# One of the four later modulation rows: its products on ScalarE, its sum by accumulating DMAs

## The chip, the cores and the metric

The kernel runs on one core of a Trainium2 chip. A core has a matrix engine (TensorE, PE in the profile), a vector engine (VectorE, DVE), an engine for pointwise functions (ScalarE, ACT), a programmable engine (GpSimd, POOL) and a sequencer that only issues transfers (SyncE, SP). Each takes its instructions strictly in order. Data lies in HBM, in the on-chip memory SBUF (128 partitions) and in PSUM, where TensorE writes its sums. DMA engines move data between HBM and SBUF, or from one place in SBUF to another; here SyncE and GpSimd issue all of them, and a transfer issued by GpSimd may also add what it brings to what already lies at its destination.

The metric is the time of one execution on the device in microseconds (us), lower being better. The profiler counts a span, from the first to the last instruction.

## The reference

```python
mod = (silu(c) @ w_mod).reshape(c.shape[0], 6, 1, -1)    # c: (1, 1024), w_mod: (1024, 6*1024)
sa, ca, ga, sb, cb, gb = (mod[:, i] for i in range(6))
h = layernorm(x) * (1 + ca) + sa                          # x: (1, 2048, 1024)
a = einsum("bsd,ed->bse", h, dft_hid_re)
b = einsum("bsd,ed->bse", h, dft_hid_im)
y = einsum("ts,bse->bte", dft_seq_re, a) - einsum("ts,bse->bte", dft_seq_im, b)
x = x + ga * y
h = layernorm(x) * (1 + cb) + sb
x = x + gb * (gelu(layernorm(h) @ w1 + b1) @ w2 + b2)     # w1: (1024, 3584), w2: (3584, 1024)
```

Six rows of 1024 numbers come from the vector c. The first two (sa, ca) are needed before the Fourier mixing, and the other four (ga, sb, cb, gb, numbered j = 2 to 5) only behind it. This case is about the row ga, j = 2.

## The kernel before

Every large product is made in 16-bit floats: each operand is split into a high half (ScalarE rounds it) and a low half (VectorE subtracts the rounded value), and three products of halves are summed. Where it can, the kernel forms seven products of sums of blocks in place of eight plain block products (Strassen's and Winograd's scheme); VectorE makes those sums.

The work follows in stages. First the rows sa and ca and the first normalization. Then the Fourier mixing along the sequence: `plain1` handles the first of four blocks of 512 outputs with 16 operands of plain products (L1123), `winograd1` the other three (tb = 1, 2, 3; L1173) with seven products of four operands each, 28 operands to a block and 84 in all, 24 matmuls to an operand. Then mixing along the hidden dimension (L1405), and the two products of the gated network (L1600, L1709).

In the second stage several streams of small tasks run beside TensorE:

- `craw` and `op`: SyncE loads pieces of the sequence matrices (L716). `split_c` turns each into an operand: the high half on ScalarE (L692), the low half on VectorE (L695). A ring of six places holds finished operands, and a place is free again when TensorE is through with its operand. Four of the seven products need sums of raw pieces first (`comb`, L727).
- `s` and `sr`: sums of the normalized input, split (L669, L672), stored in HBM by GpSimd (L676) and reloaded by SyncE (L754) into a ring of four; a reload waits until TensorE has used the place.
- `u`: the results, evicted from PSUM by ScalarE (L1192) or VectorE (L1197), combined and split (L799, L784, L787) in a staging ring of three, and stored by GpSimd (L789).
- `row`: the four later modulation rows, one after the other (`row_tasks`), and behind them, in the same stream, eight units `d_tasks` that load a part of the hidden-dimension matrices (`dre`, `dim`; L821), split it (L832 on ScalarE, L835 on VectorE) and store it (L839).

A row is made like this. Eight pieces of 128 rows of `w_mod` (128 x 1024 floats, 512 KB) are loaded by SyncE into a ring of three buffers (L547). Each is multiplied by its column of silu(c) (`scol`), one factor for each partition, and summed into `mrow` by VectorE: the first by L553, the other seven by L555. GpSimd then adds up the 128 partitions (`partition_all_reduce`, L563), VectorE scales or shifts the row (`keep`: L567 for ga, L569 for cb; `keep_b2`, L574, for the product of gb with b2), and GpSimd stores it in HBM (`put`, L577). There is one `mrow`, so the next row's first product waits until the store has read it. The first `dre` load lies over the same space and waits for the last store, that of `gbb`.

The order of all this is written down when the program is built. A small planner keeps a clock for each engine. `Task` has an engine, an estimated cost and the tasks it depends on; `push` puts tasks in a stream with a time at which they fall due; `pick` takes the task that is due first among those that could start at once on their engine, and otherwise the one that could start earliest. The operands fall due 15 us ahead of their use, the rows at fixed times 30 us apart, the units of `d_tasks` 24 us apart. `LANDS` says how long a transfer is taken to need, 2 us for a load. The planner's estimates set only the order on each engine; the waits on the chip are those of the data.

Of the kernel before, what the change touches and what calls it, by code (L numbers as in the profile page):

```python
# [12 lines left out]
AF = mybir.ActivationFunctionType  # L13
ALU = mybir.AluOpType
# [21 lines left out]
def kernel(ctx, tc, x, cre, cim, dre, dim, w1, b1, w2, b2, c, wm, out):  # L36
# [13 lines left out]
    pe, act, dve, gp, sp = nc.tensor, nc.scalar, nc.vector, nc.gpsimd, nc.sync  # L50

    pool = ctx.enter_context(tc.tile_pool(name="main", bufs=1))
# [6 lines left out]
    def mk(shape, dt, tag, bufs=1):  # L59
        cnt[0] += 1  # L60
        return pool.tile(shape, dt, tag=tag, name=f"{tag}_{cnt[0]}", bufs=bufs)
# [3 lines left out]
    def at(kb, n, dt=F32):  # L65

        w = n if dt == F32 else n // 2
        v = arena[:, int(kb * 256) : int(kb * 256) + w]
        return v if dt == F32 else v.bitcast(dt)
# [92 lines left out]
    acc = at(O_ACC, 8192).rearrange("p (b j r e) -> p b j r e", b=2, j=2, r=2)  # L162
# [54 lines left out]
    LANDS = {"dma": 2.0, "st": 4.0, ("st", "d"): 7.0, ("st", "u"): 5.0, ("st", "s"): 4.0, ("st", "z"): 4.0}  # L217
# [142 lines left out]
    def level():  # L360
        t = max(clk.values())
        for k in clk:
            clk[k] = t
        return t
# [100 lines left out]
    scol, cc = mk([P, ND], F32, "scol"), mk([P, ND], F32, "cc")  # L465
    m1 = mk([P, 6], F32, "m1")
    srep = at(216, 1024).rearrange("p (k m) -> p k m", k=ND)
    mrow, ones = at(O_AUX, 1024), at(O_SO[0], 512)
# [25 lines left out]
    def mod_rows(k, c_lo, x1):  # L494
# [43 lines left out]
        lo(1)  # L538
        dve.tensor_scalar(iu, pm, 2.0**5 / SD, None, op0=ALU.mult)

    def row_tasks(j, name):

        r = []
        for k in range(ND):
            b = at(O_AUX + 4 + 4 * (k % 3), 1024)
            l = Task(
                "dma", 1.5, lambda k=k, b=b: sp.dma_start(b, wm[:, k, j * D : (j + 1) * D]),  # L547
                [("row", j, k - 3) if k > 2 else ("row", j - 1, ND) if j > 2 else ("op", 15)], ("wm", j, k),
            )

            def mul(k=k, b=b):
                if k == 0:
                    dve.tensor_scalar(mrow, b, scol[:, 0:1], None, op0=ALU.mult)  # L553
                else:
                    dve.scalar_tensor_tensor(mrow, b, scol[:, k : k + 1], mrow, op0=ALU.mult, op1=ALU.add)  # L555

            r.append((l, Task("dve", 1.3, mul, [l.key], ("row", j, k))))
        t = [l for l, _ in r[:3]]
        for k in range(ND):
            t.append(r[k][1])  # L560
            if k + 3 < ND:
                t.append(r[k + 3][0])
        s = Task("pool", 7.0, lambda: gp.partition_all_reduce(mrow, mrow, P, RED.add), [("row", j, ND - 1)])  # L563

        def keep():
            if name == "ga":
                dve.tensor_scalar(mrow, mrow, m1[:, 3:4], None, op0=ALU.mult)  # L567
            elif name == "cb":
                dve.tensor_scalar(mrow, mrow, 1.0, None, op0=ALU.add)  # L569

        b = at(O_AUX + 4, 1024)

        def keep_b2():
            dve.tensor_tensor(mrow, mrow, b, op=ALU.mult)  # L574

        def put(n, dep, key=None):
            return Task("st", 0.0, lambda: gp.dma_start(row_d[n][:, :], mrow), [dep], key)  # L577

        if name == "gb":
            l = Task("dma", 1.5, lambda: sp.dma_start(b, b2[0].partition_broadcast(P)), [s.key])  # L580
            p = put("gb", s.key)
            m = Task("dve", 1.3, keep_b2, [l.key, p.key])
            return t + [s, l, p, m, put("gbb", m.key, ("row", j, ND))]
        if name == "sb":
            return t + [s, put(name, s.key, ("row", j, ND))]
        k_ = Task("dve", 0.9, keep, [s.key])
        return t + [s, k_, put(name, k_.key, ("row", j, ND))]
# [921 lines left out]
    for n, j in enumerate((2, 3, 4, 5)):  # L1509
        push("row", "row", row_tasks(j, {2: "ga", 3: "sb", 4: "cb", 5: "gb"}[j]), t_op(16) + 20.0 + 30.0 * n)  # L1510
# [308 lines left out]
    due, t = {}, 0.0  # L1819
# [4 lines left out]
    t = level()  # L1824
# [174 lines left out]
```

## Time and profile before

| | |
|---|---|
| median of three runs | 1976.67 us (1975.83 to 1977.92) |
| profiled execution | 1976.73 us |
| its span | 1975.0 us |
| TensorE busy | 1954.2 us, 99% |
| VectorE busy | 1422.2 us, 72% |
| ScalarE busy | 851.7 us, 43% |
| GpSimd busy | 196.3 us, 10% |
| TensorE's granted clock | 0.997 |

In the lines of the profile, L with a number is a line of the kernel. "Busy" of TensorE counts overlapping, pipelined matmuls, so that it says little on its speed. A row of the timeline gives the start of a group of instructions in microseconds from the span's start, how long the group took, the engine, the line, the operation with its output and input, how many instructions it joins, and in brackets how long the engine had been idle before, and what ended that. `SPq`, `POOLq` and the like are the sequencers that issue transfers. A row of the view of one line gives the shortest, the median and the longest duration in nanoseconds and the first and the last start; "DMA to landing" is the time from issuing a transfer until its data lies at its destination, shortest, median and longest. Almost all data on the chip lies in one tile, `arena`; names like `in_wm_dram`, `s`, `u`, `dc` and `row_ga` are tensors in HBM.

### The profile page before, as it was taken

What the parts mean: (1) busy time and instruction counts of PE and PEld (TensorE: products, weight loads), DVE (VectorE), ACT (ScalarE), POOL (GpSimd) and SP (SyncE); (2) the same over time, 40 slices, a digit from 0 to 9 for tenths busy, and PEclk for the clock granted to TensorE, in tenths of its full rate; (3) what the DMA queues carried; (4) which work ended last, traced back from release to release, by engine and by line L of the source; (5) the groups of instructions that cost most, each with busy time, mean ns of one, the idle gap of its engine ahead of it and who ended that gap; (6) DMA issues with size and microseconds to landing.
All of it is one profiled execution on the core that took longest, in us unless ns stands there. A gap on an engine that the chain in (4) does not pass through costs nothing.

```text
span 1975.0 us, 23586 instructions
## 1 busy us (share of the span) xinstructions
PE 1954.2 (99%) x9004; PEld 889.2 (45%) x9004; DVE 1422.2 (72%) x1799; ACT 851.7 (43%) x1091; POOL 196.3 (10%) x287
## 2 busy tenths in 40 slices
PE   7999999999999999999999999999999999999999
PEld 2444444444444444444444444444444444444443
DVE  5977878797985477786689998989873453553566
ACT  3843333354542255554577566456323312312311
POOL 0012212221210012211020000000000000000000
PEclk9999999999999999999999999999999999999999
DMA  9148587598778867878954554444476432432324
GB/s 385 62 142 283 183 299 289 210 330 312 268 271 335 302 241 252 288 234 298 357 177 150 189 189 164 149 149 176 171 224 197 123 102 74 130 103 67 113 75 85
DMA packets 139362, 402.41 MB, mean 204 GB/s; under 512 B 15536, under 2 KB 15536, under 8 KB 134640
## 3 DMA queue, kind: packets, MB, share of 16 engines
q1 hardware_dynamic: 111808, 307.30, 46.1%
q0 software_dynamic: 27440, 93.60, 13.3%
q8 instruction: 70, 1.15, 0.2%
q14 instruction: 44, 0.36, 0.1%
HBM read 262.95 MB, written 137.89 MB: 203 GB/s over the span
## 4 chain that ended last, share of the span: by engine, by line
PE 92%; DVE 4%; ACT 1%; issue 1%; DMA 1%; POOL 0%; SPq 0%; DVEq 0%; ACTq 0%; POOLq 0%
PE ps L1600 24%; PE ps L1173 22%; PE ps L1709 22%; PE ps L1405 15%; PE ps L1123 8%; DVE arena L409 1%; DVE arena L1755 1%; PE ps L485 1%; PE ps L1307 1%; DVE arena L422 1%; ACT arena L397 1%; DMA arena<-in_w_dram 0%; DMA arena<-in_wm_dram 0%; DVE arena L1799 0%; PE ps L484 0%
## 5 line engine op out<-in xcount | busy, mean ns | idle before, releaser
L1709 PE MATMUL ps<-arena 128*128 128x512 f16 x2352 | 511.1, 379 | 2.9 <-DVE arena L1755 1.6
L1600 PE MATMUL ps<-arena 128*128 128x512 f16 x2352 | 510.2, 379 | 0.0
L1173 PE MATMUL ps<-arena 128*128 128x512 f16 x2016 | 435.3, 379 | 0.0
L1709 PEld LDWEIGHTS <-arena 128*128 128x128 f16 x2352 | 229.8, 98 | 281.9 <-issue 4.0
L1600 PEld LDWEIGHTS <-arena 128*128 128x128 f16 x2352 | 230.2, 98 | 276.8
L1755 DVE SCALAR_TENSOR_TENSOR arena<-ps,i4c,arena 128x1024 f32<-128x1024 f32 x179 | 229.3, 1281 | 144.6 <-PE ps L1709 142.6
L1173 PEld LDWEIGHTS <-arena 128*128 128x128 f16 x2016 | 197.3, 98 | 237.9
L1405 PE MATMUL ps<-arena 128*128 128x512 f16 x1344 | 292.2, 379 | 0.0
L397 ACT ACTIVATE arena<-arena,shc 128x512 f16<-128x512 f32 (+1 forms) x115 | 116.1, 1018 | 281.6 <-PE ps L1709 189.2
L1405 PEld LDWEIGHTS <-arena 128*128 128x128 f16 x1344 | 131.5, 98 | 155.9
L1123 PE MATMUL ps<-arena 128*128 128x512 f16 x768 | 171.4, 386 | 6.8 <-ACT arena L528 3.9
L422 DVE TENSOR_TENSOR arena<-arena 128x512 f32<-128x512 f32 (+1 forms) x228 | 170.9, 753 | 4.2
L692 ACT ACTIVATE arena<-arena 128x1024 f16<-128x1024 f32 x100 | 103.8, 1050 | 152.2 <-PE ps L1173 101.1
L409 DVE SCALAR_TENSOR_TENSOR arena<-arena,shc 128x512 f16<-128x512 f32 (+1 forms) x115 | 128.6, 1122 | 37.4 <-ACT arena L397 37.1
L695 DVE SCALAR_TENSOR_TENSOR arena<-arena 128x1024 f16<-128x1024 f32 x100 | 132.7, 1345 | 22.8 <-ACT arena L692 22.6
L1626 DVE TENSOR_TENSOR arena<-arena,ps 128x512 f32<-128x512 f32 x84 | 57.6, 685 | 109.9 <-PE ps L1600 106.2
L1619 ACT ACTIVATE arena<-arena,b1s,i1c 128x512 f32<-128x512 f32 x84 | 68.3, 813 | 137.8 <-DVE arena L1626 137.8
L1123 PEld LDWEIGHTS <-arena 128*128 128x128 f16 x768 | 76.0, 99 | 102.6 <-issue 9.7
L784 ACT ACTIVATE arena<-arena 128x1024 f16<-128x1024 f32 x56 | 57.5, 1047 | 50.9 <-DMA u<-arena 19.3
L787 DVE TENSOR_TENSOR arena<-arena 128x1024 f16<-128x1024 f32 x56 | 66.8, 1217 | 14.9 <-ACT arena L784 14.9
L397 ACT ACTIVATE arena<-arena,s1c 128x512 f16<-128x512 f32 (+1 forms) x70 | 60.7, 884 | 38.1 <-DVE arena L422 26.3
L409 DVE SCALAR_TENSOR_TENSOR arena<-arena,s1c 128x512 f16<-128x512 f32 (+1 forms) x70 | 66.4, 959 | 10.8 <-ACT arena L397 10.8
(167 smaller groups left out, 1395.1 us busy)
## 6 DMA issues: line engine op xcount, KB each, us to landing
w<-arena SPq DMA_DIRECT2D x64, 512.0 KB, 4.9
arena<-w SPq DMA_DIRECT2D x119, 256.0 KB, 2.8
u<-arena POOLq DMA_DIRECT2D x56, 512.0 KB, 5.8
arena<-u SPq DMA_DIRECT2D x112, 256.0 KB, 4.2
arena<-w SPq DMA_DIRECT2D x56, 512.0 KB, 3.6
arena<-s SPq DMA_DIRECT2D x48, 512.0 KB, 6.4
arena<-in_cre_dram SPq DMA_DIRECT2D x32, 512.0 KB, 7.4
arena<-in_cim_dram SPq DMA_DIRECT2D x32, 512.0 KB, 5.0
```

Of the source, the lines that this page charges most:

```text
L397: act.activation(o[m][0], q(j), AF.Copy, **sc)
L409: dve.scalar_tensor_tensor(o[m][1], q(j), scale, o[m][0], op0=ALU.mult, op1=ALU.subtract)
L422: dve.tensor_tensor(q(d), q(a), q(b), op=op)
L692: h = Task("act", 1.15, lambda: act.activation(o[:, :, 0], s2, AF.Copy, scale=SC), list(deps) + free)
L695: dve.scalar_tensor_tensor(o[:, :, 1], s2, SC, o[:, :, 0], op0=ALU.mult, op1=ALU.subtract)
L1123: pe.matmul(bank_of(d_), hleft(d_, s, kp, a), cop(n)[:, s, b], start=(kp == 0 and s == 0 and a == 0 and b == 0), stop=(kp == 7 and s == 1 ...
L1173: pe.matmul(bank_of(st + ch), left, cop(n)[:, s, b], start=(start and kp == 0 and s == 0 and a == 0 and b == 0), stop=(kp == 3 and s == 1 ...
L1405: pe.matmul(bank_of(bk), up(N)[:, c_, a], dp(n)[:, c_, w], start=(start and ri == 0 and c_ == 0 and i == 0), stop=(ri == 1 and c_ == 3 and ...
L1600: pe.matmul(ps.rearrange("p (k t) -> p k t", k=4), w1c[:, m, s, a, d * P : (d + 1) * P], zc(m)[:, b, :, d, :], start=(start and d == 0 and ...
L1619: act.activation(dst, src, AF.Gelu_apprx_tanh, scale=inv, bias=b1s[:, 2 * p + j : 2 * p + j + 1])
L1709: pe.matmul(t[:, j], hidc[:, c_, m, a, k * P : (k + 1) * P], w2c[:, m, c_, w], start=(start and c_ == 0 and n == 0), stop=(c_ == 1 and n = ...
L1755: lambda: dve.scalar_tensor_tensor(dst, ps[b], inv, dst, op0=ALU.mult, op1=ALU.add), kp[b],
```

## The change

For the row j = 2 alone, `scaled` takes the place of the eight VectorE instructions. ScalarE multiplies a piece by its column of silu(c): the first into `mrow`, the other seven in place in their buffers. GpSimd then issues, for each of the seven, a DMA that adds the buffer to `mrow`. Each waits for its product and for the DMA before it. A buffer is free for its next load when the DMA that reads it has landed. The planner is told 1.1 us for a product on ScalarE, 1 us for issuing an accumulating DMA and 8 us for its landing. The row's all-reduce, scaling and store, and the other three rows, are made as before.

```diff
+    def scaled(acc, b, k, name, dep):
+
+        key = lambda k: (*name, k)
+        LANDS[key(k)] = 8 if k else 0.0
+        if k == 0:
+            return [Task("act", 1.1, lambda: act.activation(acc, b, AF.Copy, scale=scol[:, k : k + 1]), [dep], key(k))]
+        p = (*name, k, "b")
+        return [
+            Task("act", 1.1, lambda: act.activation(b, b, AF.Copy, scale=scol[:, k : k + 1]), [dep], p),
+            Task("pool", 1.0, lambda: gp.dma_start(acc, b, accum_op=ALU.add), [key(k - 1), p], key(k)),
+        ]
+
     def row_tasks(j, name):
...
                 [("row", j, k - 3) if k > 2 else ("row", j - 1, ND) if j > 2 else ("op", 15)], ("wm", j, k),
             )
 
+            if j in (2,):
+                r.append((l, scaled(mrow, b, k, ("row", j), l.key)))
+                continue
+
             def mul(k=k, b=b):
...
-            r.append((l, Task("dve", 1.3, mul, [l.key], ("row", j, k))))
+            r.append((l, [Task("dve", 1.3, mul, [l.key], ("row", j, k))]))
         t = [l for l, _ in r[:3]]
         for k in range(ND):
-            t.append(r[k][1])
+            t += r[k][1]
             if k + 3 < ND:
                 t.append(r[k + 3][0])
```

Sixteen lines are added, so lines from about 560 on have numbers larger by 12, and from 565 on by 16: L695 becomes L711, L1173 becomes L1189. As built, the orders on all engines but TensorE differ from those before from about the middle of the stores of s until the last `dc` loads; TensorE's order is the same.

## The prediction

> **What bounds the kernel now.** I read the page's busy shares first, then the chain that ended last, cut to the stretch in which the change works (the queue orders of the two programs agree before about 185 us and after about 610 us, and TensorE's order is the same throughout), then VectorE's, GpSimd's and SyncE's timelines there.
>
> ```profile
> span 1975.0 us, 23586 instructions
> PE 1954.2 (99%) x9004; PEld 889.2 (45%) x9004; DVE 1422.2 (72%) x1799; ACT 851.7 (43%) x1091; POOL 196.3 (10%) x287
> 184.83 27.63 PE ps L1123 x128
> 212.46 435.12 PE ps L1173 x2016
> 647.58 12.52 PE ps L1405 x58
> ```
>
> The chain there is TensorE alone, without a gap: 2016 matmuls in 435.12 us. They use 84 operands, prepared by ScalarE (L692) and VectorE (L695), so one operand lasts 435.12 / 84 = 5.18 us, and operand j (from 0) is wanted at 212.46 + 5.18 j. Nothing that this change frees can shorten that row; it can only lengthen it, by making an operand late. So what counts is how early operands are ready now. I counted the L695 rows of the timeline to number them; three of the latest:
>
> ```profile
> 390.98 1.23 DVE L574 TENSOR_TENSOR arena<-arena 128x1024 f32<-128x1024 f32 x1 [9.37 <-issue]
> 393.26 1.22 DVE L695 SCALAR_TENSOR_TENSOR arena<-arena 128x1024 f16<-128x1024 f32 x1
> 435.40 1.22 DVE L695 SCALAR_TENSOR_TENSOR arena<-arena 128x1024 f16<-128x1024 f32 x1
> 442.42 1.22 DVE L695 SCALAR_TENSOR_TENSOR arena<-arena 128x1024 f16<-128x1024 f32 x1 [1.14 <-ACT arena L692]
> ```
>
> They are operands 36, 44 and 45, ended at 394.5, 436.6 and 443.6 and wanted at 398.9, 440.4 and 445.6: 4.4, 3.8 and 2.0 us to spare. Ahead of the first, VectorE stood 9.37 us for the last row's all-reduce; the other two lie behind pieces of the `dre` splits (L835), which follow the rows in their stream. The rows' lateness is passed on to these places.
>
> **The change, part by part.** Off VectorE go one product of L553 and seven of L555; onto ScalarE come eight activations, priced as the nearest (L692, also 1024 elements).
>
> ```profile
> L553 DVE TENSOR_SCALAR arena<-arena,scol x4: 743/746/754, 217.5 to 349.0; 128x1024 f32<-128x1024 f32 x4
> L555 DVE SCALAR_TENSOR_TENSOR arena<-arena,scol x28: 1275/1283/1285, 220.4 to 370.1; 128x1024 f32<-128x1024 f32 x28
> L692 ACT ACTIVATE arena<-arena x100: 1039/1056/1058, 28.3 to 616.5; 128x1024 f16<-128x1024 f32 x100
> ```
>
> That is 0.75 + 7 x 1.28 = 9.7 us less on VectorE and 8 x 1.06 = 8.4 us more on ScalarE, both beside a full TensorE: worth nothing by themselves. ScalarE's cover is the operand lead; were it gone, at most 8.4 us would show.
>
> The seven accumulating DMAs are issued by GpSimd, each after the one before has landed. The trace has no such DMA into SBUF; the nearest add 512 KB into HBM from the same queue:
>
> ```profile
> L1808 POOL DMA_DIRECT2D out_dram<-arena x8: 845/1066/1537, 1463.9 to 1490.5; - x8
> DMA to landing us min/median/max: 6.4/10.1/13.1
> ...
> L1783 POOL DMA_DIRECT2D out_dram<-arena x4: 1191/1198/1201, 1940.6 to 1962.8; - x4
> DMA to landing us min/median/max: 5.6/5.7/5.8
> ```
>
> 5.7 us one by one, up to 13.1 in a burst. I take 9: ours are one by one, but beside busy DMA engines. In GpSimd's order two go between the stores of s, the other five behind the last:
>
> ```profile
> 211.49 1.07 POOL L676 DMA_DIRECT2D s<-arena  x2 [0.82 <-DVE arena L672]
> 235.17 7.02 POOL L563 PARTITION_ALL_REDUCE arena<-arena  x1 [22.61 <-DVE arena L555]
> 295.10 7.28 POOL L563 PARTITION_ALL_REDUCE arena<-arena  x1
> 331.67 7.00 POOL L563 PARTITION_ALL_REDUCE arena<-arena  x1 [28.34 <-DVE arena L555]
> 379.17 8.42 POOL L563 PARTITION_ALL_REDUCE arena<-arena  x1
> ...
> 388.00 0.55 POOL L577 DMA_DIRECT2D row_gb<-arena  x1 [0.41 <-POOL arena L563]
> 392.62 0.55 POOL L577 DMA_DIRECT2D row_gbb<-arena  x1 [4.08 <-DVE arena L574]
> ```
>
> From 212.6, and some 3 us for stores pushed back, the five end at 216 + 5 x 9 = 261 and the all-reduce at 268 (now 242.2). VectorE comes to the row's scaling (L583 after) at about 266, and the next operand behind it, 16, is wanted at 295.3: no cost at 5.7 (251.5), nor at 13.1 (288.5). SyncE's queue waits too: the reloads of the ring wait for landings, with raw c loads behind that are wanted from 254 on, and the stores of u behind the chain have a ring of three. All this stays inside the lead.
>
> [...] In the trace issuing took 0.85 to 1.54 us (L1808).
>
> The cost comes later, from where the planner has put the three other rows. SyncE's order:
>
> ```profile
> 305.74 1.08 SPq L754 DMA_DIRECT2D arena<-s  x2
> 341.99 0.33 SPq L754 DMA_DIRECT2D arena<-s  x1
> ...
> 395.61 0.56 SPq L821 DMA_DIRECT2D arena<-in_dre_dram  x1
> ...
> 430.05 10.68 SPq L754 DMA_DIRECT2D arena<-s  x3
> ```
>
> Row sb's last wm load now stands behind the reload at 305.74, cb's behind the one at 341.99; these wait for TensorE. Loads of wm landed thus:
>
> ```profile
> L547 SPq DMA_DIRECT2D arena<-in_wm_dram x4: 407/423/454, 342.4 to 352.8; - x4
> DMA to landing us min/median/max: 5.1/8.8/9.9
> ...
> L547 SPq DMA_DIRECT2D arena<-in_wm_dram x4: 328/328/367, 358.0 to 366.5; - x4
> DMA to landing us min/median/max: 3.4/4.8/7.1
> ```
>
> Row sb: 306.5 + 7 (between the medians) + 1.3 = 314.8, all-reduce to 322 (now 302.4). Row cb: 342.4 + 8.8 + 1.3 = 352.5; its all-reduce now follows three stores of u, whose halves and two operands lie on VectorE in between (5 x 1.2 = 6): 359 to 366 (now 331.7 to 338.7). Then 0.7 for the scaling and nine instructions of 1.2 to gb's first product, which ends at 377 (now 349.8, below).
>
> ```profile
> 349.03 0.74 DVE L553 TENSOR_SCALAR arena<-arena,scol 128x1024 f32<-128x1024 f32 x1
> 367.48 3.92 DVE L555 SCALAR_TENSOR_TENSOR arena<-arena,scol 128x1024 f32<-128x1024 f32 x3
> ...
> 234.98 6.69 DVE L695 SCALAR_TENSOR_TENSOR arena<-arena 128x1024 f16<-128x1024 f32 x2
> ```
>
> gb now takes 349.0 to 371.4, 22.4 us. With three buffers and lighter transfers (4.8) I get 16.5: last product 393.6. Its all-reduce starts at once, to 400.7, and holds VectorE, as at 234.98: 6.69 for two instructions of 1.22, so 4.3 us. One combination and operand 36 lie there: 393.6 + 1.2 + 4.3 + 1.2 = 400.3, wanted at 398.9. **Stall 1.4 us.**
>
> Then four instructions and the b2 product to 406.3, the store of gbb (0.2 + 2.9 to land), and the first `dre` load, which waits for it:
>
> ```profile
> DMA to landing us min/median/max: 2.9/2.9/6.9
> ...
> DMA to landing us min/median/max: 5.6/7.8/9.9
> ...
> 403.47 0.68 DVE L835 SCALAR_TENSOR_TENSOR arena<-arena 128x512 f16<-128x512 f32 x1
> ...
> 418.16 1.22 DVE L695 SCALAR_TENSOR_TENSOR arena<-arena 128x1024 f16<-128x1024 f32 x1
> ```
>
> The first line is of L577, the second of L821. Load at 410 (now 395.6), landed 418; VectorE is free at 420.7 after 12 instructions. The splits up to the next operand took 403.47 to 419.4, 15.9: so 436.6 or a little more. That is operand 43, wanted at 435.2 plus the 1.4 lost: **0.5**. Operand 44 follows after four instructions and a ScalarE half, 5.9: 443.1 against 440.4 + 1.9: **0.8**. The second `dre` load stands behind the second reload of that block (430.05) and lands at 441, in time. Operand 45 takes 5.7 more, 448.8 against 445.6 + 2.7: **0.5**; operand 46 6.7 more, 455.5 against 450.7 + 3.2: **1.6**. Operand 47 is in time again. The sum is 4.8 us: 1976.73 in the profiled execution (1975.0 of span and 1.7 around it; the median of the three runs is 1976.67) becomes 1981.5.
>
> ```profile
> L835 DVE SCALAR_TENSOR_TENSOR arena<-arena x32: 678/1216/1227, 403.5 to 576.3; 128x1024 f16<-128x1024 f32 x24, 128x512 f16<-128x512 f32 x8
> ...
> 680.43 0.60 SPq L1524 DMA_DIRECT2D arena<-row_ga  x1
> ```
>
> The finished rows are read back only at 680, and the `dre` chain, which ends at 577.5 and would end some 15 to 20 us later, still frees its buffer before 600 for loads wanted from 647.58 on: no cost.
>
> **Rivals.** *Not slower (0.38).* Every stall above is a difference of two long sums. With wm landings of 4.8 in row cb too, each step is 4 us earlier, operand 36 is done at 396.3 before 398.9, and about 1 us is left: 1976.7 to 1979. For it: VectorE's own 9.7 us less. Against it: the spare time is 2 to 4 us already. It decides when gb's last product ends before 392.
> *Slow accumulation (0.10).* If a step takes over 14 us, 216 + 5 x 14 + 7 = 293 and VectorE stands at the scaling while operand 16 is wanted at 295.3; each us more costs 5. At 15.5 it is about 8 us, with later stalls 1988. Against it: 13.1 is the most seen, in a burst. [...]
> *Faster, or nothing done (0.02).* A gain needs a gap in TensorE's row, and there is none; if VectorE still ends each row by waiting, its freed time is idle time.
>
> **How the numbers follow.** Stalls of 3 to 9 us 0.50, slow accumulation 0.10, not slower 0.38, faster 0.02. The bound between slower and same is 0.2%, 4 us, about what a measurement of this kernel can tell from no change; I count 0.02 of the first case below it. So slower 0.58, same 0.40, faster 0.02. The range runs from no stall, 1976.0, to landings of 8.8 also in gb (4 us on each of two rounds, near 1985) and row ga at 13.1 (some 4 more): 1989. The likeliest case alone: 1979.7 to 1986.
>
> **What would show it.** Right: idle TensorE before L1189 (now L1173) between 395 and 460 us, ended by L711; VectorE waiting at L590 and before L711 there; an all-reduce of row gb ending near 400; accumulations 6 to 13 us apart; nothing changed after 650 but the shift. Wrong: no idle TensorE at all; gb's all-reduce before 392; or the gap near 295, behind L583.

## The result and the profile after

The changed kernel takes 1981.3 us (median of 11 runs, 1977.6 to 1984.15) against 1976.65 us (median of 11, 1974.31 to 1979.18): a ratio of 1.0023, with a 95% interval of 1.0015 to 1.0031. It is slower by 0.23%, 4.65 us; forecast were 1981.5 us and slower. The profiled execution took 1980.01 us. The first lines are from its page, the others from TensorE's timeline:

```profile
span 1978.1 us, 23589 instructions
PE 1952.5 (99%) x9004; PEld 888.4 (45%) x9004; DVE 1411.3 (71%) x1791; ACT 859.8 (43%) x1099; POOL 199.8 (10%) x294
```

```profile
212.59 233.63 PE L1189 MATMUL ps<-arena 128*128 128x512 f16 x1081
447.93 5.34 PE L1189 MATMUL ps<-arena 128*128 128x512 f16 x24 [1.71 <-DVE arena L711]
453.75 196.78 PE L1189 MATMUL ps<-arena 128*128 128x512 f16 x911 [0.48 <-DVE arena L711]
650.38 9.88 PE L1421 MATMUL ps<-arena 128*128 128x512 f16 x45
```

VectorE has 10.9 us less work and ScalarE 8 us more (9.7 and 8.4 were forecast). The row of 2016 matmuls, which had no gap before, has two, of 1.71 and 0.48 us, at operands 45 and 46, both ended by VectorE's low halves (L711). From the first matmul of L1189 to the first of L1421 it takes 650.38 - 212.59 = 437.79 us in place of 435.12: 2.67 us more. That stage length is the yardstick below. It is finer than the whole time, since the moment at which the stage begins differs between executions: 209.47 to 212.59 us over all profiles, and these two are of kernels whose orders agree up to there (e9_splits_behind below, and after).

GpSimd's timeline, the view of L550 (the accumulating DMA) and VectorE's timeline show the rows on their way:

```profile
L550 POOL DMA_DIRECT2D arena<-arena x7: 848/871/903, 186.4 to 249.5; - x7
...
DMA to landing us min/median/max: 4.5/6.8/10.1
```

```profile
260.97 6.15 POOL L579 PARTITION_ALL_REDUCE arena<-arena  x1
315.15 7.00 POOL L579 PARTITION_ALL_REDUCE arena<-arena  x1 [43.56 <-DVE arena L571]
356.48 7.28 POOL L579 PARTITION_ALL_REDUCE arena<-arena  x1
391.93 7.01 POOL L579 PARTITION_ALL_REDUCE arena<-arena  x1 [6.30 <-DVE arena L571]
```

```profile
392.88 5.55 DVE L711 SCALAR_TENSOR_TENSOR arena<-arena 128x1024 f16<-128x1024 f32 x1
...
437.69 1.22 DVE L711 SCALAR_TENSOR_TENSOR arena<-arena 128x1024 f16<-128x1024 f32 x1
442.11 0.69 DVE L851 SCALAR_TENSOR_TENSOR arena<-arena 128x512 f16<-128x512 f32 x1 [3.20 <-ACT arena L848]
...
446.66 1.22 DVE L711 SCALAR_TENSOR_TENSOR arena<-arena 128x1024 f16<-128x1024 f32 x1
...
452.48 1.23 DVE L711 SCALAR_TENSOR_TENSOR arena<-arena 128x1024 f16<-128x1024 f32 x1
```

The four all-reduces start at 261, 315, 356 and 392 us; before, it was 235, 295, 332 and 379. The gaps come from the last block above. At 438.9 VectorE is through with operand 44 (the row of 437.69). Next in its order is the first split of the second `dre` unit (L851), and it stands 3.20 us for that. The low halves of operands 45 and 46 (446.66, 452.48) stand behind it. What it waits for is ScalarE's half of that split (L848), and ScalarE stands for the unit's load itself, with the high half of operand 45 (L708) behind it. ScalarE's timeline:

```profile
441.45 1.58 ACT L848 ACTIVATE arena<-arena 128x512 f16<-128x512 f32 x2 [7.25 <-DMA arena<-in_dre_dram]
...
444.74 1.05 ACT L708 ACTIVATE arena<-arena 128x1024 f16<-128x1024 f32 x1
```

That high half is done at 445.8, when TensorE wants it (212.59 + 45 x 5.18 = 445.7); the low half at 447.9. So one late load holds both engines that make operands. SyncE's timeline, first of the kernel after, then of the one before, tells why the load was late:

```profile
425.16 5.50 SPq L770 DMA_DIRECT2D arena<-s  x2
430.76 0.55 SPq L837 DMA_DIRECT2D arena<-in_dre_dram  x1
```

```profile
414.94 1.42 SPq L821 DMA_DIRECT2D arena<-in_dre_dram  x1
```

In the order of after it stands behind two more reloads of s that wait for TensorE to free their places, and goes out at 430.76, 16 us later than before. The chain of waits has how long it took to land:

```profile
430.76 10.61 DMA arena<-in_dre_dram
```

The same load took 9.4 us in the kernel before; at that, by an estimate, it would have landed at 440.2 here, still behind 438.9. So it is mostly the late issue that counts.

### The profile page after: what moved, and what is told of

Read it like the earlier page. It is cut to its first block, busy times and chain, and to the rows that moved or that the text cites. A ratio compares the mean times of both kernels' runs of the same rounds, so it can differ in the third digit from the quotient of the medians.

```text
span 1978.1 us, 23589 instructions
## 1 busy us (share of the span) xinstructions
PE 1952.5 (99%) x9004; PEld 888.4 (45%) x9004; DVE 1411.3 (71%) x1791; ACT 859.8 (43%) x1099; POOL 199.8 (10%) x294
## 4 chain that ended last, share of the span: by engine, by line
PE 86%; DVE 8%; DMA 2%; issue 2%; ACT 1%; POOL 1%; SPq 0%; DVEq 0%; ACTq 0%; POOLq 0%
PE ps L1616 25%; PE ps L1725 23%; PE ps L1189 16%; PE ps L1421 15%; PE ps L1139 5%; DVE arena L711 1%; DMA arena<-in_wm_dram 1%; DVE arena L660 1%; DMA arena<-in_dre_dram 1%; DVE arena L661 1%; PE ps L485 1%; POOL arena L579 1%; PE ps L1323 1%; DVE arena L1771 1%; DVE arena L663 1%
## 5 line engine op out<-in xcount | busy, mean ns | idle before, releaser
L1189 PE MATMUL ps<-arena 128*128 128x512 f16 x2016 | 435.8, 379 | 2.2 <-DVE arena L711 2.2
L1189 PEld LDWEIGHTS <-arena 128*128 128x128 f16 x2016 | 197.3, 98 | 240.5 <-issue 3.0
L1421 PE MATMUL ps<-arena 128*128 128x512 f16 x1344 | 292.2, 379 | 0.0
L1421 PEld LDWEIGHTS <-arena 128*128 128x128 f16 x1344 | 131.5, 98 | 155.9
L708 ACT ACTIVATE arena<-arena 128x1024 f16<-128x1024 f32 x100 | 103.4, 1050 | 143.1 <-PE ps L1189 99.4
L711 DVE SCALAR_TENSOR_TENSOR arena<-arena 128x1024 f16<-128x1024 f32 x100 | 130.8, 1327 | 37.8 <-ACT arena L708 37.8
L803 DVE TENSOR_TENSOR arena<-arena 128x1024 f16<-128x1024 f32 x56 | 66.8, 1219 | 17.7 <-ACT arena L800 17.7
```

The costliest lines, as they stand in the source:

```text
L708: h = Task("act", 1.15, lambda: act.activation(o[:, :, 0], s2, AF.Copy, scale=SC), list(deps) + free)
L711: dve.scalar_tensor_tensor(o[:, :, 1], s2, SC, o[:, :, 0], op0=ALU.mult, op1=ALU.subtract)
L1189: pe.matmul(bank_of(st + ch), left, cop(n)[:, s, b], start=(start and kp == 0 and s == 0 and a == 0 and b == 0), stop=(kp == 3 and s == 1 ...
L1421: pe.matmul(bank_of(bk), up(N)[:, c_, a], dp(n)[:, c_, w], start=(start and ri == 0 and c_ == 0 and i == 0), stop=(ri == 1 and c_ == 3 and ...
```

## The experiments

Two things can have moved that load: the real time that the sums need, or the order that the planner wrote when it was told of 8 us for each. "Lost" in this table is the stage length less 435.12 us, from TensorE's timeline in the run's profile; the ratio is to the kernel before on the same chip.

| run | edit | lost, us | ratio (95% interval) |
|---|---|---|---|
| after | | 2.67 | 1.0023 (1.0015 to 1.0031) |
| e1_no_sum | after without the seven sums | 4.69 | 1.0026 (1.0015 to 1.0036) |
| e2_dve_same_plan | order of after, row ga on VectorE | 4.96 | 1.0025 (1.0014 to 1.0037) |
| e7_no_gb_reduce | after without gb's all-reduce | 4.75 | 1.0020 (1.0011 to 1.0028) |
| b1_gb_reduce_twice | before, gb's all-reduce twice | 4.03 | 1.0023 (1.0014 to 1.0032) |
| e5_dve_add | ScalarE's products, VectorE's sums | 5.74 | 1.0033 (1.0020 to 1.0046) |
| e6_unit1_later | after, second `dre` unit loaded later | 0.29 | 1.0041 (1.0029 to 1.0053) |
| e9_splits_behind | after, that unit's splits behind operand 46 | 0.00 | 0.9998 (0.9989 to 1.0007) |
| e3_lands2 | after, planner told 2 us a sum | 9.73 | 1.0065 (1.0052 to 1.0078) |
| e4_sum_twice | after, each sum issued twice | 21.83 | 1.0138 (1.0118 to 1.0158) |
| e10_before_plan | work of after, planned as before | 15.93 | 1.0086 (1.0072 to 1.0099) |
| b2_plan_128, b6_plan_133 | before, another figure for the planner | 0.00, 0.00 | 1.0000 (0.9991 to 1.0009), 0.9996 (0.9988 to 1.0005) |

### Is it the sums, or the order? e1_no_sum and e2_dve_same_plan

```diff
-            Task("pool", 1.0, lambda: gp.dma_start(acc, b, accum_op=ALU.add), [key(k - 1), p], key(k)),
+            Task("pool", 1.0, lambda: None, [key(k - 1), p], key(k)),
```

> The seven accumulating DMAs are left out (row ga is then only its first product, so the result is not the reference's); the order on every queue, as the planner wrote it with 8 us a landing, is that of the kernel after. Theory A (the written order costs it: the last wm loads of rows sb and cb stand on SyncE behind reloads that wait for TensorE, so gb ends late whatever row ga does): row ga is done by 240, yet sb's all-reduce still starts near 315, gb's near 390, and TensorE still idles 2 to 6 us between 395 and 460; 1979 to 1983. Rival B (the real landings of the sums hold the rows up, or their traffic slows the loads): no idle TensorE, 1976 to 1977.5.

In the second run the planner's tasks stay, and what they issue is changed:

```diff
-            return [Task("act", 1.1, lambda: act.activation(acc, b, AF.Copy, scale=scol[:, k : k + 1]), [dep], key(k))]
+            return [Task("act", 1.1, lambda: dve.tensor_scalar(acc, b, scol[:, 0:1], None, op0=ALU.mult), [dep], key(k))]
...
-            Task("act", 1.1, lambda: act.activation(b, b, AF.Copy, scale=scol[:, k : k + 1]), [dep], p),
-            Task("pool", 1.0, lambda: gp.dma_start(acc, b, accum_op=ALU.add), [key(k - 1), p], key(k)),
+            Task("act", 1.1, lambda: None, [dep], p),
+            Task("pool", 1.0, lambda: dve.scalar_tensor_tensor(acc, b, scol[:, k : k + 1], acc, op0=ALU.mult, op1=ALU.add), [key(k - 1), p], key(k)),
```

> The planner plans the kernel after, but what is issued for row ga are the eight VectorE instructions of before, at the places where ScalarE's first product and the seven sums stood. No ScalarE product, no accumulating DMA, result as the reference's. Theory A (written order): as after, 1979 to 1983, gb's all-reduce near 390. Rival B (the DMAs' landings or traffic) and rival C (ScalarE's 8 x 1.13 us push back the high halves): 1976 to 1977.5, no idle TensorE between 395 and 460.

TensorE's timeline of the first:

```profile
209.83 233.26 PE L1189 MATMUL ps<-arena 128*128 128x512 f16 x1080
444.07 0.38 PE L1189 MATMUL ps<-arena 128*128 128x512 f16 x1 [0.97 <-ACT arena L708]
446.15 203.65 PE L1189 MATMUL ps<-arena 128*128 128x512 f16 x935 [1.71 <-DVE arena L711]
649.64 50.67 PE L1421 MATMUL ps<-arena 128*128 128x512 f16 x234
```

In the second the two gaps are 1.24 and 1.71 us, at the same places. Without one accumulating DMA, and even without ScalarE's products, the loss is there, at the same operand 45 (1080 matmuls are 45 operands of 24), in both halves now: its high half (L708) comes 0.97 us late, its low half 1.71 us after that. The high half is late because ScalarE, too, stood for the load: it went out at 428.00, and ScalarE's half of its split (L848) let VectorE go on only at 440.33, after 5.50 us. So the sums' landings, their traffic and ScalarE's 8 us are not what costs; the written order is. One number of the first expectation missed: row ga's all-reduce began at 258.22, not before 240, since in GpSimd's order it stands behind stores of u, whoever made the row.

### Is it row gb's lateness? e7_no_gb_reduce, b1_gb_reduce_twice, e5_dve_add

```diff
-        s = Task("pool", 7.0, lambda: gp.partition_all_reduce(mrow, mrow, P, RED.add), [("row", j, ND - 1)])
+        s = Task("pool", 7.0, lambda: gp.partition_all_reduce(mrow, mrow, P, RED.add) if j < 5 else None, [("row", j, ND - 1)])
```

> The kernel after without the all-reduce of row gb (gb is then only a sum over the rows of one partition, so the result is not the reference's). The row is stored some 7 us earlier, VectorE isn't held, and the first dre load goes out 5 to 7 us earlier. Theory (lateness is handed from row gb to the dre units): idle TensorE under 0.5 us, 1976 to 1978. Rival (places behind row gb lose their slack by something else, ScalarE or traffic): as after, 1979 to 1982.

The theory fell here. SyncE's timeline of that run:

```profile
401.92 0.56 SPq L837 DMA_DIRECT2D arena<-in_dre_dram  x1
...
422.21 5.50 SPq L770 DMA_DIRECT2D arena<-s  x2
427.80 0.99 SPq L837 DMA_DIRECT2D arena<-in_dre_dram  x1
```

The first `dre` load goes out at 401.92 instead of 410.49, 8.6 us earlier. Of these, 3.0 us are the stage, which began at 209.63 instead of 212.59; counted from its start the first load is 5.6 us earlier, and the second not at all: 218.17 us behind the start in both, since it stands behind the reloads, and these go at TensorE's pace. VectorE stood 6.11 us for it instead of 3.20, and 4.75 us are lost. What was gained ahead was waited away at that place.

The 5.6 us need not be the all-reduce's: in e9_splits_behind, which has the all-reduce and the same order up to there, the first load is as early (192.3 us behind the stage's start, 197.9 in after). Over the profiles of after and of four runs with its order there (e1, e2, e7, e9) the first load goes out 192.3 to 197.9 us behind the start, and the second at 218.2 each time.

In the kernel before, on the other hand, where the second load goes out 16 us earlier, a late row is enough:

```diff
-        s = Task("pool", 7.0, lambda: gp.partition_all_reduce(mrow, mrow, P, RED.add), [("row", j, ND - 1)])
+        s = Task("pool", 7.0, lambda: [gp.partition_all_reduce(mrow, mrow, P, RED.add) for _ in range(1 + (j == 5))], [("row", j, ND - 1)])
```

> The kernel before, with row gb's all-reduce issued twice in a row (gb is then 128 times too large, so the result is not the reference's): row gb is 7 us later by nothing else, no ScalarE product and no accumulating DMA. Theory (a late gb row is enough, since operands 36, 44, 45 have 2 to 4.4 us to spare): VectorE held twice, operand 36 ready at 400 to 402 for 398.9, and TensorE idles 1.5 to 6 us between 398 and 460; 1978 to 1983. Rival (it needs the sums or their order): 1976 to 1977.5.

TensorE's timeline:

```profile
397.44 41.60 PE L1173 MATMUL ps<-arena 128*128 128x512 f16 x192 [0.84 <-DVE arena L695]
441.30 5.34 PE L1173 MATMUL ps<-arena 128*128 128x512 f16 x24 [2.25 <-DVE arena L695]
447.10 201.96 PE L1173 MATMUL ps<-arena 128*128 128x512 f16 x935 [0.46 <-DVE arena L695]
```

Operand 36 is the first that is late, 44 and 45 follow: the three tight places that the prediction quoted of the kernel before. So the mechanism that it described is real; it is just not the one that ended last in the order of after.

The third run keeps ScalarE's products, with no accumulating DMA and so a short row ga:

```diff
-        LANDS[key(k)] = 8 if k else 0.0
+        LANDS[key(k)] = 0.0
...
-            Task("pool", 1.0, lambda: gp.dma_start(acc, b, accum_op=ALU.add), [key(k - 1), p], key(k)),
+            Task("dve", 1.3, lambda: dve.tensor_tensor(acc, acc, b, op=ALU.add), [key(k - 1), p], key(k)),
```

> Row ga's products stay on ScalarE, but VectorE adds them (seven TENSOR_TENSOR of 1.22 us) and no accumulating DMA is issued; the planner is told so, and its order of the three other rows is again near that of before. Theory (ScalarE's 8 products of 1.13 us cost nothing; the loss needs row ga to be long): gb's all-reduce between 375 and 385, no idle TensorE over 0.5 us, 1976 to 1978. Rival C (the products on ScalarE hold up the high halves): idle TensorE between 185 and 300 behind L708, over 1979.

Wrong as well: row gb's all-reduce starts at 375.76, earlier than before (379.17), there is no late high half, and yet 5.74 us are lost. TensorE's and VectorE's timelines:

```profile
454.26 5.34 PE L1189 MATMUL ps<-arena 128*128 128x512 f16 x24 [3.32 <-DVE arena L711]
```

```profile
448.44 0.69 DVE L851 SCALAR_TENSOR_TENSOR arena<-arena 128x512 f16<-128x512 f32 x1 [4.81 <-ACT arena L848]
```

It is the third `dre` unit here, loaded at 436.14, for which VectorE stands 4.81 us with operand 46 behind it; another 1.42 us are lost at operand 38, behind the splits of the first unit. Neither a sum nor a late row is needed: a `dre` split ahead of an operand that is wanted soon, and its load behind the reloads, do it.

### The place itself: e9_splits_behind and e6_unit1_later

```diff
-        first = split((0,), slice(0, 1), [l.key]) + split((1, 5), slice(2, 4), [l.key])
+        first = split((0,), slice(0, 1), [l.key] + ([("op", 62)] if n == 1 else [])) + split((1, 5), slice(2, 4), [l.key])
```

The kernel counts the 16 operands of the first block too, so its `op` 62 is operand 46.

> The kernel after, with one dependency more in the plan: the second dre unit is loaded when it was, but its first split waits in the plan for operand 46 and so stands behind operands 45 and 46 in VectorE's order. Theory (all of the idle TensorE is VectorE waiting for that unit's load with 45 and 46 behind it, and the sums of row ga cost nothing): idle TensorE under 0.5 us between 395 and 460; the last unit ends before 605, so that the dc loads behind 650 wait for under 1 us; 1976 to 1978, not told from before. Rival (the units are as late as in the run that loaded the second one later): 2 us or more of idle TensorE behind 650 for dc, 1979 to 1984.

SyncE's, VectorE's and TensorE's timelines of it:

```profile
427.63 1.17 SPq L837 DMA_DIRECT2D arena<-in_dre_dram  x1
```

```profile
436.23 1.22 DVE L711 SCALAR_TENSOR_TENSOR arena<-arena 128x1024 f16<-128x1024 f32 x1
...
439.75 1.22 DVE L711 SCALAR_TENSOR_TENSOR arena<-arena 128x1024 f16<-128x1024 f32 x1
441.48 0.69 DVE L851 SCALAR_TENSOR_TENSOR arena<-arena 128x512 f16<-128x512 f32 x1 [0.51 <-ACT arena L848]
```

```profile
209.47 435.28 PE L1189 MATMUL ps<-arena 128*128 128x512 f16 x2016
```

The load goes out when it did in the run without gb's all-reduce (427.80), and its split starts no earlier (441.48, there 440.19). But VectorE makes operands 45 and 46 meanwhile, at 436.23 and 439.75, and ScalarE their high halves ahead of the split as well. No gap is left: 1976.38 us, ratio 0.9998. All engines' orders are those of after up to that split. With the sums, ScalarE's products and the long row ga all in place, the change costs nothing measurable. That settles the cause: the two engines waiting for that load with operands 45 and 46 behind them. How much of it is ScalarE's wait and how much VectorE's, this run can't tell, since it moves both.

Loading the unit later instead moves the lateness on:

```diff
-        l = Task("dma", 2.9, lambda: sp.dma_start(b, dri[ri][:, c_::4, :]), [("dd", n - 1)] if n else [("row", 5, ND)])
+        l = Task("dma", 2.9, lambda: sp.dma_start(b, dri[ri][:, c_::4, :]), [("dd", n - 1)] + ([("op", 62)] if n == 1 else []) if n else [("row", 5, ND)])
```

> The kernel after with one dependency more in the plan: the second dre unit is loaded only once operand 46 is ready, so that its splits stand behind operands 45 and 46 and no more ahead of them. Theory (the idle TensorE of 1.7 and 0.5 us sits at operands 45 and 46 because VectorE waits for that unit's late load in front of them): none of it left there, 1976 to 1978, if the units, then some 20 us later, still end before their buffer is wanted. Rival (VectorE lacks time there whatever stands ahead; or the loss is noise of the start): idle TensorE moves to neighbouring operands, 1979 to 1983.

TensorE's waits behind 600 us:

```profile
PE ps L1421 <- DMA arena<-dc: 5.1, 2, 3.5
```

The gaps at 45 and 46 are gone (0.29 us lost). But the units now run from 446.52 to a last load at 598.46, and TensorE waits 5.1 us for `dc` in the next stage: 1985.02 us. The prediction had put "no cost" on a `dre` chain 15 to 20 us later. With the last load at 573.28, as in the kernel after, that held; 25 us more broke it.

### What late sums would cost: e3_lands2, e4_sum_twice, e10_before_plan

```diff
-        LANDS[key(k)] = 8 if k else 0.0
+        LANDS[key(k)] = 2 if k else 0.0
```

> The kernel after with the planner told 2 us instead of 8 for the landing of a sum. The scaling of row ga (L583) then stands in VectorE's order ahead of operand 8, wanted near 254. Theory A with the measured step of 8 to 10 us a sum: the seventh sum lands at 248 to 255, the all-reduce ends at 255 to 262, VectorE stands there, TensorE idles 3 to 12 us near 254 to 270, and 1980 to 1990 with what comes later. Rival (the loss comes only from the long landing that the planner was told, and a plan with a short one is as good as before): 1976 to 1977.5, no idle TensorE near 254.

VectorE's timeline, then TensorE's:

```profile
251.58 0.75 DVE L583 TENSOR_SCALAR arena<-arena,m 128x1024 f32<-128x1024 f32 x1 [17.95 <-POOL arena L579]
```

```profile
253.52 20.66 PE L1189 MATMUL ps<-arena 128*128 128x512 f16 x95 [1.99 <-DVE arena L711]
278.30 39.23 PE L1189 MATMUL ps<-arena 128*128 128x512 f16 x168 [4.11 <-DMA arena<-s]
```

VectorE stands 17.95 us for row ga at the scaling, as the slow case of the prediction has it, and TensorE 1.99 us behind it, less than the 3 to 12 us expected. The larger gap is one that I had not listed: 4.11 us for a reload of s.

```diff
-            Task("pool", 1.0, lambda: gp.dma_start(acc, b, accum_op=ALU.add), [key(k - 1), p], key(k)),
+            Task("pool", 1.0, lambda: [gp.dma_start(acc, b, accum_op=ALU.add) for _ in range(2)], [key(k - 1), p], key(k)),
```

> Each accumulating DMA is issued twice, one after the other (the sum counts seven products twice, so the result is not the reference's); the planner's order is that of after. The five sums behind the stores of s take 85 us instead of 45: the last lands near 296, the all-reduce ends near 303, and the scaling stands ahead of operand 16, wanted at 295.5. By the prediction's third case (from 14 us a step on, each us costs 5): idle TensorE of 8 to 14 us near 295 to 310 behind L583, and rows sb, cb, gb some 30 us later with more idle behind: 1988 to 2015. Rival (sums are pipelined by the queue and a second one costs far less than the first): the scaling before 285, 1979 to 1984.

The total, 2003.1 us, lies in the expected range, but not by the expected way. TensorE's timeline, then the chain of waits ahead of the second gap:

```profile
218.04 70.48 PE L1189 MATMUL ps<-arena 128*128 128x512 f16 x318 [4.35 <-ACT arena L1118]
300.23 115.93 PE L1189 MATMUL ps<-arena 128*128 128x512 f16 x529 [11.71 <-DMA arena<-s]
```

```profile
276.39 0.54 DMA arena<-arena
276.93 5.57 DMA u<-arena
...
283.70 1.23 DVE arena L803
...
289.49 0.33 SPq L732
...
289.91 10.27 DMA arena<-s
```

The sums hold GpSimd's queue, so a store of u waits; the staging ring is full, so VectorE waits at a u half (L803) with operands behind it; then SyncE waits with a load for its place, and a reload of s stands behind that. The first gap begins at the queue too: ScalarE stands 11.93 us, until 216.45, for a store of s, with evictions (L1118) behind. The prediction had said of these queues "All this stays inside the lead". At the sums' real length it does. At twice that, the queue past GpSimd gives out before the scaling does.

The last of these puts the work of after at the places of the order of before:

```diff
                 if k == 0:
-                    dve.tensor_scalar(mrow, b, scol[:, 0:1], None, op0=ALU.mult)
+                    (act.activation(mrow, b, AF.Copy, scale=scol[:, 0:1]) if j == 2 else dve.tensor_scalar(mrow, b, scol[:, 0:1], None, op0=ALU.mult))
+                elif j == 2:
+                    act.activation(b, b, AF.Copy, scale=scol[:, k : k + 1])
+                    gp.dma_start(mrow, b, accum_op=ALU.add)
```

> The work of the kernel after at the places of the order of before: the planner is told that row ga's products are VectorE instructions, and ScalarE's product and the accumulating DMA are issued where they stood. All seven sums stand on GpSimd behind the stores of s. Theory: 213 + 7 x 8.5 = 272 for the last landing, the all-reduce ends at 279, and the scaling stands in VectorE's order ahead of an operand wanted at 270: 8 to 15 us of idle TensorE there, and with the stores of u behind the all-reduce 1985 to 2000 in all. Rival (the order alone costs, what is done in it does not): 1976 to 1978.

GpSimd's and TensorE's timelines:

```profile
228.61 0.87 POOL L556 DMA_DIRECT2D arena<-arena  x1 [8.06 <-DMA arena<-arena]
...
258.35 0.86 POOL L556 DMA_DIRECT2D arena<-arena  x1 [4.29 <-ACT arena L787]
262.98 6.13 POOL L566 PARTITION_ALL_REDUCE arena<-arena  x1 [3.77 <-DMA arena<-arena]
```

```profile
271.08 5.12 PE L1176 MATMUL ps<-arena 128*128 128x512 f16 x23 [1.99 <-DVE arena L698]
283.79 12.46 PE L1176 MATMUL ps<-arena 128*128 128x512 f16 x48 [7.58 <-DMA arena<-s]
```

With the queue to themselves the sums come (258.35 - 228.61) / 5 = 5.9 us apart, so the all-reduce ended at 269.1, not at 279. Even so the stage loses 15.93 us (1992.99 us in all). The order of before can't take these sums; the planner's 8 us saved 11 to 13 of those 16 us and cost the small gap at operands 45 and 46.

### Does any other order lose? b2_plan_128 and b6_plan_133

```diff
-            r.append((l, Task("dve", 1.3, mul, [l.key], ("row", j, k))))
+            r.append((l, Task("dve", 1.28, mul, [l.key], ("row", j, k))))
```

> The kernel before, the same work to the instruction; only the planner's figure for a row product on VectorE is 1.28 us instead of 1.3. The orders of VectorE, ScalarE, GpSimd and SyncE change. Theory (any order but the one of before gives up some of the 2 to 4 us that its tight places have to spare): 0.5 to 6 us of idle TensorE between 390 and 460, 1977.5 to 1983. Rival (it needs a row made late): 1976 to 1977.5 and no idle TensorE.

> As the one with 1.28, with 1.33 us instead of 1.3 told to the planner; the same work. Theory: 0.5 to 6 us of idle TensorE between 390 and 460, 1977.5 to 1983. Rival: 1976 to 1977.5 and no idle TensorE.

Both lose nothing (1975.69 and 1975.95 us), though the orders of VectorE, ScalarE, GpSimd and SyncE all changed. So it was wrong that any order but that of before gives up the spare time. What costs is one bad placement, and an order may have it or not.

## Why the prediction was right, and where not

The direction, the size (4.8 us forecast, 4.65 measured in the medians) and the stretch, 395 to 460 us, came out. Its own steps:

| step | forecast | measured in after |
|---|---|---|
| row ga's all-reduce | 261 to 268 | 260.97 to 267.1 |
| row sb's all-reduce | 315 to 322 | 315.15 to 322.2 |
| row cb's all-reduce | 359 to 366 | 356.48 to 363.8 |
| gb's last product, all-reduce | 393.6, to 400.7 | 391.8, to 398.9 |
| VectorE held by it | 4.3 | 5.55 - 1.22 = 4.3 |
| operand 36 ready | 400.3, 1.4 late | 398.4, no gap |
| first `dre` load | 410 | 410.49 |
| operands 43, 44 ready | 436.6, 443.1: 0.5 and 0.8 late | before 438.9, no gap |
| second `dre` load lands | 441, "in time" | 441.4, VectorE waiting since 438.9 |
| operands 45, 46 ready | 448.8, 455.5: 0.5 and 1.6 late | 447.9, 453.7: gaps of 1.71 and 0.48 |

The sums came 8.4 us apart from 215.80 to 249.54 (9 taken) and landed after 4.5 to 10.1 us. The last landed at 255.0, and the all-reduce began only at 260.97, behind three stores of u (258.39 to 260.40). It began 48.4 us behind the stage's start, and just so in the run without sums (258.22 - 209.83). So the agreement in the first line of the table is luck: the stores set that time, not the sums.

Issuing a sum took 0.85 to 0.90 us, no longer than the 0.85 to 1.54 us that the prediction quoted. Why some landings took up to 10.1 us, no run here shows.

Two steps failed. For operand 36 I drew the line at 392 for gb's last product. The first product ended at 374.2, not 377, and the others took 17.6 us, not 16.5; so the last ended at 391.8, and the 1.4 us did not come. By that line the rival "not slower" had won, and yet the kernel is slower. The second is the greater: "lands at 441, in time". I had asked only whether the load was in time for TensorE, and not when VectorE and ScalarE would come to its split. VectorE came early: the splits of the first unit took 15.9 us as forecast but began at 418.3, not 420.7, and operands 43 and 44 were not held up. So it stood there. The row's lateness, from which I derived all five stalls, is not what costs: with the first `dre` load 5.6 us earlier, 4.75 us are lost all the same, and with the split behind operand 46 nothing is. Five small stalls were forecast, and there is one place, with two. What was right of the mechanism is that the new order's late loads reach the operands around 45; that 4.8 and 4.65 us agree is luck.

The profiled execution of after lost 2.67 us in the stage, three runs with its order there lost 4.69 to 4.96. The next section has the difference. Which of the two happened in each timed run (1977.6 to 1984.15) isn't seen.

## What to carry to other kernels

When an order written by a planner changes, look for instructions that wait for a transfer and have work behind them that is wanted soon; ask when the engine comes to them, and not only when the result is needed. A transfer that stands behind another which waits for a slow engine keeps that engine's pace: hastening what comes before it buys nothing, as the 218.2 us of five profiles show. The mend was to put the two pressed operands ahead of the wait, on both engines, and not to shorten the long step; and since TensorE's row had no gap to give, the mended kernel, with 9.7 us less on VectorE, is only as fast as the one before.

## What was not expected of the hardware

Two short gaps cost nearly twice their length here. Of the run without sums (e1_no_sum), TensorE in stretches of 2 us (columns: stretch, length, busy time and matmuls, granted clock, share of the DMA engines, GB/s):

```profile
444.00:446.00 2.00, 0.38 (x1) 1.00 0.79 244
446.00:448.00 2.00, 1.85 (x7) 0.79 1.03 379
448.00:450.00 2.00, 2.00 (x6) 0.50 0.96 367
450.00:452.00 2.00, 2.00 (x10) 0.86 0.39 158
```

TensorE was idle for 0.97 and 1.71 us with one matmul between, and then ran at half its clock: by these shares 2 x (0.21 + 0.50 + 0.14) = 1.7 of the 4.69 us lost are that. The gaps of the kernel after, 1.71 and 0.48 us with 24 matmuls between, left the clock at 1.00, and so did a gap of 3.32 us in the run with VectorE's sums. Behind one of 3.55 us in the run with the unit loaded later, 12 matmuls took 2.75 us, 0.23 each, near the 0.22 at 1.00 (24 in 5.34 us in the kernel after), so that the clock was not halved there either; 4.11 us in the run planned with 2 us a sum brought 0.50 again for over 6 us. This is how 2.67 us in one profile and 4.7 to 5.0 in three others come from the same order: in the three (e1, e2, e7) TensorE went on with the high half of operand 45 16.1 to 16.3 us after the load went out, where that half was done after 15.0 in the kernel after (so the load took, by an estimate, 11.6 to 11.9 us to land, not 10.61), the idle time was 0.5 to 0.8 us longer, and the half clock (0.50 from 448 to 450 in each) came on top.

The half clock followed stretches of 3.05 us (443.1 to 446.15 in the run without sums) to 3.33 us with a matmul in them, in these three runs, and yet it did not follow 3.55 us of idleness without one. So the length of the stretch does not decide it by itself; what does, no run here shows.

Lastly, the accumulating DMA into SBUF, of which the profile before has no row: 512 KB landed in 4.5 to 10.1 us, and one by one with GpSimd's queue free they came 5.9 us apart, close to the 5.7 us in which the adding transfers of the same size into HBM landed (L1783).
